# A fourth q/k buffer with earlier loads, the small constant added in another copy, and x sums spread over more periods

## The chip, the cores and the metric

One core of one Trainium2 chip. The metric is the device time of one execution in microseconds (us). The kernel before takes 1035.89 us, the median of three runs (1034.39, 1035.89, 1038.68).

## The reference

Attention over 4 batches, 8 heads, 576 tokens, head size 64, and behind it two gated layers on the 2304 x 512 result:

```python
scores = q @ k.T / 8 ; causal mask ; bias = min(-(cum[q] - cum[k]), 0), cum = cumsum(max(s, 0))
attn = exp(scores - rowmax) ; attn = attn / (sum(attn) + 1e-9) ; x = attn @ v
x = (sigmoid(x @ w_gate) * (x @ w_val)) @ w_out
out = ((x @ w_a) * (x @ w_b)) @ w_out2
```

The gated layers have 512 inputs and 1536 inner columns. Their weights arrive as float64 and are converted to float32 on the chip by integer operations.

## The kernel before, in words

The kernel has two stages. The first 207 us or so are attention (`attention()`), the rest are the two gated layers (`mlps()`). Each stage records its operations in a `Schedule` with a name, an engine, a duration, what it depends on, a due time ("prio") and, for some, a buffer that it takes and one that it gives back. The attention stage is emitted with `in_order=True`: of all operations whose predecessors have been emitted, the one with the lowest due time comes next. So the due times, in periods of `HT` = 6.1 us for one head, are an order written out by hand for every engine and for the DMA queues of SP (nc.sync), ACT (nc.scalar) and POOL (nc.gpsimd). An engine runs its instructions in that order and waits where an operand is not there yet. The second stage is emitted by a planner from its own durations; the change does not touch it, except that one operation of its first list (`rc`) is shorter.

For head i the operations that matter here are, with the lines of the profile:

- `lqk` (L380, SP): load q and k of the head, 288 KB, into `r_t[i % NR2]`; with three buffers it must wait until `hq1`, `hk1`, `lok` and `loq` of head i-3 have read the old contents.
- `hq1`, `hk1` (L532, L533, ACT): round q and k to the short format into `o_t[i % 4]`.
- `hk2` (L534, ACT's queue) and `hq2` (L535, SP's queue): copy the rounded k and q to the other half of the partitions, 144 KB each; the profile shows both as o<-o.
- `lok` (L536, DVE) and `loq` (L538, POOL): what rounding left of k and q. `lok` needs the transfer of `hk2`.
- `S` (L557, L562, PE): scores of the head in two groups, 0 and 1, one PSUM tile `ps_g` after the other. `mx` (L570, DVE): row maxima, which free `ps_g`. `mT` (L577, PE), `mc` (L579, ACT) and `md` (L581, ACT's queue): turn the maxima, copy them to `mr_t[i % 3]` and write them as a row of the operand.
- `ST` (L594, L595, PE): scores transposed, less the maximum. `ex` (L600, ACT): exponentials. `cs` (L616, POOL): the causal edge.

For two heads together (pair j): `lv` (L384, L385, SP) loads v; `pv` and `pd` (L641, L654, PE) are the product with v and the sums; `xc` (L663, ACT) and `dc` (L665, DVE) copy both out of PSUM; `dc` writes `dn`. Then the sums go through DRAM (`dw` L676, `dr` L677) into a small tile `t` of 128 x 12 (`sc` in the profile), `rc` adds 1e-9 (L669) and takes the reciprocal (L670), and `rd`, `rb`, `xm` (L682, POOL) and `xd` (L684) scale x and write it to `x_sb`. The last pairs' `dr` to `xd` run in the second stage.

Beside that the attention stage has the first weights to load and convert (`LOADS`: L194 on SP's queue, L215 on ACT, L216, L218, L220 and L223 on DVE; a tuple gives the period of each step) and their sums (L255), and it prepares the first x operands of the second stage: `xs` (L318, DVE) sums of x parts, `xh` (L321, ACT) their rounded half, `xl` (L324, DVE) the rest. `AT_S`, `AT_H` and `AT_L` give the period of each. Two staging tiles (`stg`) hold S1 to S4.

## Time and profile before

| | |
|---|---|
| median of three runs | 1035.89 us |
| the profiled execution, its own time | 1037.12 us |
| its span, first to last instruction | 1035.1 us |
| busy: PE, DVE, ACT, POOL | 1009.5, 700.1, 466.2, 385.4 us |
| mean granted TensorE clock | 0.995 of full speed |

The profiled execution is 1.23 us above the median, and 2.0 us of it lie around the span. Below, "PE" is TensorE, "DVE" VectorE, "ACT" ScalarE, "POOL" GpSimd and "SP" SyncE. In the timeline a row gives the start in us, the duration, the engine and line, the operation, its tiles, and in brackets how long the engine sat idle before it and what released it. A queue's own rows are named SPq and ACTq.

### The profile page before, as it was taken

To read this page: it belongs to the slowest core of one execution; us is meant where nothing else is said; L and a number is where in the kernel's file an instruction comes from. 1 tells how busy PE (TensorE), PEld (TensorE's weight loads), DVE (VectorE), ACT (ScalarE), POOL (GpSimd) and SP (SyncE) were. 2 spreads that over 40 slices of the span, in tenths; PEclk is the share of its full clock that TensorE was granted. 3 is DMA by queue.
4 is the path that set the end of the run, shared out by engine and by line. 5 is a ranking of instruction groups with operands and counts; after the bars stand their busy time and mean duration, and the time that the engine had idled before them with its cause. 6 is when DMAs were issued, how large, how long until landed. Compare 5 with 4: busy or idle time off the path is not lost.

```text
span 1035.1 us, 17118 instructions
## 1 busy us (share of the span) xinstructions
PE 1009.5 (98%) x6160; PEld 912.6 (88%) x6160; DVE 700.1 (68%) x1146; ACT 466.2 (45%) x891; POOL 385.4 (37%) x388
## 2 busy tenths in 40 slices
PE   6999899999999999999999999999999999999998
PEld 4777676699999999998888899999999999888886
DVE  7787789789689655679855339867876566932222
ACT  3676566465555445555343235334333334432221
POOL 5677688452356334433200013244533432400000
PEclk9999999999999999999999999999999999999999
DMA  5667778341234222445653332124432244544333
GB/s 158 184 172 206 192 190 198 100 152 67 103 128 139 91 102 84 163 165 199 207 157 98 121 129 92 58 90 142 128 103 87 102 154 171 179 137 137 112 103 102
DMA packets 93586, 139.76 MB, mean 135 GB/s; under 512 B 16215, under 2 KB 54863, under 8 KB 93502
## 3 DMA queue, kind: packets, MB, share of 16 engines
q1 hardware_dynamic: 89234, 133.03, 41.0%
q10 hardware_dynamic: 2988, 4.95, 1.8%
q0 software_dynamic: 1280, 0.70, 0.3%
q8 instruction: 48, 0.79, 0.3%
q14 instruction: 36, 0.29, 0.1%
HBM read 85.53 MB, written 33.45 MB: 115 GB/s over the span
## 4 chain that ended last, share of the span: by engine, by line
PE 79%; DVE 11%; DMA 5%; issue 2%; ACT 2%; POOL 1%; SPq 0%; ACTq 0%; DVEq 0%; POOLq 0%
PE ps L290 24%; PE ps L292 24%; PE ps L291 24%; PE ps_x L641 2%; DVE nm L570 2%; PE ps_g L557 2%; DMA vx<-in_vm_dram 2%; PE ps_x L654 1%; DMA o<-o 1%; DVE o L536 1%; DVE s L824 1%; DVE hs L318 1%; DVE rg L324 1%; ACT pt L600 1%; DMA r<-in_qk_dram 1%
## 5 line engine op out<-in xcount | busy, mean ns | idle before, releaser
L290 PE MATMUL ps<-rg,wk 128*128 128x384 f32 (+2 forms) x1128 | 381.9, 339 | 2.6 <-DVE s L824 2.6
L292 PE MATMUL ps<-rg,wk 128*128 128x384 f32 (+2 forms) x1128 | 381.0, 338 | 0.0
L290 PEld LDWEIGHTS ps<-rg,wk 128*128 128x128 f32 x1128 | 211.8, 188 | 9.0 <-DVE s L824 4.3
L292 PEld LDWEIGHTS ps<-rg,wk 128*128 128x128 f32 x1128 | 211.8, 188 | 3.8
L824 DVE TENSOR_TENSOR s<-ps,s 128x384 f32<-128x384 f32 x216 | 119.1, 553 | 114.4 <-PE ps L292 66.2
L291 PE MATMUL ps<-x_sb,wk 128*128 128x384 f32 x576 | 192.5, 334 | 0.0
L291 PE MATMUL ps<-rg,wk 128*128 128x384 f32 (+2 forms) x552 | 188.5, 341 | 0.0
L837 POOL TENSOR_TENSOR hs<-s,s 128x384 f32<-128x384 f32 x72 | 87.8, 1219 | 265.7 <-issue 92.9
L821 ACT COPY s<-ps 128x384 f32<-128x384 f32 x216 | 103.6, 480 | 182.6 <-PE ps L292 181.4
L268 POOL TENSOR_TENSOR wk<-raw,wk 128x512 fp32r<-128x512 f32 x96 | 125.3, 1332 | 148.0 <-DMA rg<-hd 101.8
L904 DVE TENSOR_TENSOR rg<-rg 128x512 fp32r<-128x512 f32 (+1 forms) x120 | 79.9, 670 | 111.4 <-ACT rg L903 108.5
L903 ACT CAST rg<-rg 128x512 fp32r<-128x512 f32 (+1 forms) x120 | 68.6, 578 | 146.1 <-DMA rg<-hd 113.3
L291 PEld LDWEIGHTS ps<-x_sb,wk 128*128 128x128 f32 x576 | 108.1, 188 | 0.1
L291 PEld LDWEIGHTS ps<-rg,wk 128*128 128x128 f32 x552 | 103.7, 188 | 3.6
L570 DVE TENSOR_REDUCE nm<-ps_g 128x1 f32<-128x512 f32 (+4 forms) x154 | 74.1, 531 | 19.6 <-PE ps_g L562 19.0
L290 PE MATMUL ps<-rg,rg 128*128 128x512 f32 (+1 forms) x228 | 86.1, 378 | 0.0
L291 PE MATMUL ps<-rg,rg 128*128 128x512 f32 (+1 forms) x228 | 86.1, 378 | 0.0
L292 PE MATMUL ps<-rg,rg 128*128 128x512 f32 (+1 forms) x228 | 86.1, 378 | 0.0
L215 ACT ACTIVATE mag<-raw 128x512 f32<-128x512 f32 x72 | 48.4, 673 | 55.2 <-DVE raw L223 31.4
L220 DVE SCALAR_TENSOR_TENSOR raw<-raw,u 128x512 int32<-128x512 int32 x72 | 62.5, 868 | 4.1
L218 DVE SCALAR_TENSOR_TENSOR u<-raw,u 128x512 int32<-128x512 int32 x72 | 60.8, 844 | 1.5
L616 POOL TENSOR_SCALAR_AFFINE_SELECT pt<-pt 128x256 f32<-128x256 f32 (+1 forms) x96 | 42.0, 458 | 52.9 <-ACT pt L600 49.3
(120 smaller groups left out, 1503.0 us busy)
## 6 DMA issues: line engine op xcount, KB each, us to landing
hd<-hs SPq DMA_DIRECT2D x72, 384.0 KB
rg<-hd SPq DMA_DIRECT2D x72, 256.0 KB
raw<-in_moe_w_out_dram SPq DMA_DIRECT2D x24, 512.0 KB
r<-in_qk_dram SPq DMA_DIRECT2D x32, 288.0 KB
rg<-hd SPq DMA_DIRECT2D x72, 128.0 KB
raw<-in_moe_w_gate_dram SPq DMA_DIRECT2D x12, 512.0 KB
raw<-in_moe_w_val_dram SPq DMA_DIRECT2D x12, 512.0 KB
raw<-in_moe_w_a_dram SPq DMA_DIRECT2D x12, 512.0 KB
```

The source lines that it names most:

```text
L218: ("DVE", 0.65, lambda: nc.vector.scalar_tensor_tensor(out=u, in0=parts(n, m)[1], scalar=-0x40000000, in1=u, op0=ALU.bitwise_and, op1=ALU. ...
L220: ("DVE", 0.65, lambda: nc.vector.scalar_tensor_tensor(out=parts(n, m)[1], in0=parts(n, m)[0], scalar=29, in1=u, op0=ALU.logical_shift_rig ...
L268: return lambda: nc.gpsimd.tensor_tensor(out=wcols(n, a, w, 1), in0=src(), in1=f32(wcols(n, a, w, 0)), op=ALU.subtract)
L290: nc.tensor.matmul(out=outp, lhsT=wh, rhs=xh, start=start and e == 0, stop=False, skip_group_check=True)
L291: nc.tensor.matmul(out=outp, lhsT=wh, rhs=xl, start=False, stop=False, skip_group_check=True)
L292: nc.tensor.matmul(out=outp, lhsT=wl, rhs=xh, start=False, stop=stop and e == n - 1, skip_group_check=True)
L570: nc.vector.tensor_reduce(out=nm[0:n, c:c + 1], in_=ps[0:n, p0:p0 + nk], axis=AX.X, op=ALU.max)
L821: op((x,) + key, "ACT", ACT_P, lambda x=x: nc.scalar.copy(out=s(x), in_=bank("X")), [P(p)], end(p) - 10, acq=("s", key + (x,)))
L824: return lambda: nc.vector.tensor_tensor(out=s(x), in0=bank(b_), in1=s(x), op=ALU.add)
L837: op(("h2",) + key, "Pool", PTT, lambda: nc.gpsimd.tensor_tensor(out=half(1), in0=s("s4"), in1=s("s2"), op=ALU.mult), [("c22",) + key, (g[ ...
L903: op(("hh",) + key, "ACT", 0.17 + 0.00083 * N, lambda hs=hs, N=N: nc.scalar.copy(out=hs()[:, 0, 0:N], in_=f32(hs()[:, 1, 0:N])), [("hl",) ...
L904: op(("ho",) + key, "DVE", 0.157 + 0.00104 * N, lambda hs=hs, N=N: nc.vector.tensor_tensor(out=hs()[:, 1, 0:N], in0=f32(hs()[:, 1, 0:N]), ...
```

## The change

q and k get four load buffers, and from head 3 on the load is due one period (6.1 us) earlier; the loads of heads 3 and 4 stand at the same place near the start. `mr_t` goes from three tiles to two, so `mc` of a head waits for `md` of two heads before. `dc` becomes an addition of 1e-9 on its way out of PSUM, and the addition in `rc` is dropped. The last conversion step of one weight piece (L223) moves from period 27 to 26; the sum S2 moves from 27.1 to 28, its rounded half from 28 to 29 and its rest from 29 to 31.01; A22's rounded half from 29 to 28; S1's rest from 28 to 29; S4's rounded half from 30.1 to 31 and A12's from 31 to 30.

```diff
@@ -349,7 +349,7 @@
             SUP = 1.0 / scale
             R1 = D + 2 * NR
             KB = R1 + 2
-            NO, NR2, NX, NPT = 4, 3, 4, 4
+            NO, NR2, NX, NPT = 4, 4, 4, 4
             QD, QV = 384, 128
             P0 = [0, 576, 1024, 1344, 1536]
             CQ1, CK1 = 0, 640
@@ -368,7 +368,7 @@
             mkb = tile1([128, 448], BF16, "mkb")
             nm_t = [tile1([128, 8], FP32, f"nm{i}") for i in range(4)]
             stg = [tile1([128, 2 * NP], FP32, f"stg{i}") for i in range(2)]
-            mr_t = [tile1([NC, 128], F32R, f"mr{i}") for i in range(3)]
+            mr_t = [tile1([NC, 128], F32R, f"mr{i}") for i in range(2)]
             o_t = [tile1([128, CK1 + S], F32R, f"o{i}") for i in range(NO)]
             p_t = [tile1([128, 2 * S], F32R, f"o2_{i}") for i in range(3)]
             rel = tile1([128, 2, S], F32R, "rel")
@@ -491,7 +491,7 @@
             op("mkb", "ACT", 0.7, masks_b, ["masks"], -280)
             op("mkc", "ACT", 0.2, masks_c, ["mkb"], -279)
             op("busy", "PE", 8.0, busy, ["mkb"], -270, acq=("F", "busy"), rel=("F", "busy"))
-            for j in range(NR2):
+            for j in range(3):
                 op(("lqk", j), "SP", 0.6, lambda j=j: load_qk(j), ["s"], (-290, -259.5, -258.5)[j], lat=3.0)
             for j in range(NO):
                 op(("sel", j), "SP", 1.3, lambda j=j: selectors(o_t[j]), ["selc"] + [("ms", j) if j < 3 else "more"] * (j > 0), (-260, -257, -208, 0.5)[j], lat=2.2)
@@ -520,25 +520,25 @@
                 b, h = divmod(i, H)
                 t0 = HT * i
                 o, o2, r, pt = o_t[i % NO], p_t[i % 3], r_t[i % NR2], pt_t[i % NPT]
-                nm, mr = nm_t[i % 4], mr_t[i % 3]
+                nm, mr = nm_t[i % 4], mr_t[i % 2]
                 k1, q1, k2, q2 = o[:, CK1:CK1 + S], o[:, CQ1:CQ1 + S], o2[:, S:2 * S], o2[:, 0:S]
                 up, dn = slice(0, D), slice(D, 2 * D)
                 done = [("ST", i - NO, c) for c in range(NC)] + [("S", i - NO, g) for g in range(2)]
                 done2 = [("ST", i - 3, c) for c in range(NC)]
 
-                if i >= NR2:
+                if i >= 3:
                     op(("lqk", i), "SP", 0.7, lambda: load_qk(i),
-                       [(w, i - NR2) for w in ("hq1", "hk1", "lok", "loq")], t0 - 4 * HT + 3.9, lat=3.0)
-                op(("hq1", i), "ACT", 0.65, lambda: nc.scalar.copy(out=q1[up], in_=r[up]), [("lqk", i)] + done, (-251, -247, -209.7)[i] if i < NR2 else t0 - 3 * HT + 5.2)
-                op(("hk1", i), "ACT", 0.65, lambda: nc.scalar.copy(out=k1[up], in_=r[dn]), [("lqk", i)] + done, (-251, -247, -209.7)[i] if i < NR2 else t0 - 3 * HT + 5.22)
-                op(("hk2", i), "ACT", 0.7, lambda: nc.scalar.dma_start(out=f32(k2[dn]), in_=f32(k1[up])), [("hk1", i)] + done2, (-209.8, -209.6, -8.55)[i] if i < NR2 else t0 - 2 * HT + 0.35)
-                op(("hq2", i), "SP", 0.5, lambda: nc.sync.dma_start(out=f32(q2[up]), in_=f32(q1[up])), [("hq1", i)] + done2, (-208.5, -207.5, -206)[i] if i < NR2 else t0 - 2 * HT + 0.1)
+                       [(w, i - NR2) for w in ("hq1", "hk1", "lok", "loq")], max(t0 - 5 * HT + 3.9, 0.01 * i - 2.23), lat=3.0)
+                op(("hq1", i), "ACT", 0.65, lambda: nc.scalar.copy(out=q1[up], in_=r[up]), [("lqk", i)] + done, (-251, -247, -209.7)[i] if i < 3 else t0 - 3 * HT + 5.2)
+                op(("hk1", i), "ACT", 0.65, lambda: nc.scalar.copy(out=k1[up], in_=r[dn]), [("lqk", i)] + done, (-251, -247, -209.7)[i] if i < 3 else t0 - 3 * HT + 5.22)
+                op(("hk2", i), "ACT", 0.7, lambda: nc.scalar.dma_start(out=f32(k2[dn]), in_=f32(k1[up])), [("hk1", i)] + done2, (-209.8, -209.6, -8.55)[i] if i < 3 else t0 - 2 * HT + 0.35)
+                op(("hq2", i), "SP", 0.5, lambda: nc.sync.dma_start(out=f32(q2[up]), in_=f32(q1[up])), [("hq1", i)] + done2, (-208.5, -207.5, -206)[i] if i < 3 else t0 - 2 * HT + 0.1)
                 op(("lok", i), "DVE", 0.9, lambda: nc.vector.tensor_tensor(
                     out=k2[up], in0=r[dn], in1=f32(k2[dn]), op=ALU.subtract), [("hk2", i)], (-8.7, -8.3)[i] if i < 2 else t0 - HT - 0.3)
                 op(("loq", i), "DVE" if i < 2 else "Pool", 0.9 if i < 2 else 1.4, lambda: (nc.vector if i < 2 else nc.gpsimd).tensor_tensor(
                     out=q2[dn], in0=r[up], in1=f32(q1[up]), op=ALU.subtract), [("hq1", i)] + done2, -151 + 2 * i if i < 2 else t0 - HT + 1.45)
 
-                if i >= NR2:
+                if i >= 3:
                     op(("rel", i), "SP", 0.5, lambda: nc.sync.dma_start(out=f32(q1[R1:KB + 1]), in_=relq_d[i]), relst + done, t0 - 3 * HT + 0.05, lat=2.2)
                     op(("relk", i), "Pool", 0.6, lambda: nc.gpsimd.dma_start(out=f32(k1[D:R1]), in_=f32(rel[i:NR * BH:BH])), ["sums"] + done, t0 - 3 * HT + 1.4, lat=2.2)
 
@@ -571,13 +571,13 @@
                                 out=nm[0:n, c:c + 1], in_=ps[0:n, p0:p0 + nk], axis=AX.X, op=ALU.max)
 
                     op(("S", i, g), "PE", (0.7, 0.65)[g], scores,
-                       [("rel", i), ("hq1", i), ("hk1", i), ("sel", i % NO), "mkc", "pads"] + [("relk", i)] + ([("relq", i, j) for j in range(NR)] if i < NR2 else []),
+                       [("rel", i), ("hq1", i), ("hk1", i), ("sel", i % NO), "mkc", "pads"] + [("relk", i)] + ([("relq", i, j) for j in range(NR)] if i < 3 else []),
                        first_at[g] if first_at and first_at[g] else t0 + (3.5 - 2 * HT, -HT)[g], acq=to)
                     op(("mx", i, g), "DVE", (1.4, 1.1)[g], maxima, [("S", i, g), ("mT", i - 4), "pads"], (first_at[g] or 6.1) + 0.05 if first_at else t0 + (4.3 - 2 * HT, 0.7 - HT)[g], rel=to)
                 op(("mT", i), "PE", 0.15, lambda: nc.tensor.transpose(sc.get("t", ("m", i))[0:NC, 0:128], nm[:, 0:NC], idf),
                    [("mx", i, 0), ("mx", i, 1), "masks"], (-8.7, -8.4)[i] if i < 2 else t0 - HT + 3.4, acq=("t", ("m", i)))
                 op(("mc", i), "ACT", 0.25, lambda: nc.scalar.copy(out=mr, in_=sc.get("t", ("m", i))[0:NC, 0:128]),
-                   [("mT", i), ("md", i - 3)], (-8.7, -8.4)[i] + 0.05 if i < 2 else t0 - HT + 3.55, rel=("t", ("m", i)))
+                   [("mT", i), ("md", i - 2)], (-8.7, -8.4)[i] + 0.05 if i < 2 else t0 - HT + 3.55, rel=("t", ("m", i)))
                 op(("md", i), "ACT", 0.4, lambda: nc.scalar.dma_start(
                     out=f32(o[KB:KB + 1, CQ1:CQ1 + 640]), in_=f32(mr)), [("mc", i)] + done, (-8.7, -8.4)[i] + 0.06 if i < 2 else t0 - HT + (3.93, 5.21)[i % 2], lat=2.2)
 
@@ -662,11 +662,10 @@
                 for u, (a, z) in enumerate(((0, QV), (QV, S))):
                     op(("xc", j, u), "ACT", (0.2, 0.5)[u], lambda a=a, z=z: nc.scalar.copy(out=x[:, a:z], in_=sc.get(*pxk)[:, QD + a:QD + z]),
                        [("pv", j, u), ("xd", j - NX)], t0 + (4 - u * (j < NH // 2 - 1)) * HT + 3.9)
-                op(("dc", j), "DVE", 0.5, lambda: nc.vector.tensor_copy(out=dn, in_=sc.get(*pxk)[:, 0:QD]),
+                op(("dc", j), "DVE", 0.5, lambda: nc.vector.tensor_scalar(dn, sc.get(*pxk)[:, 0:QD], 1e-9, None, ALU.add),
                    [("pd", j), ("dw", j - 1), ("xc", j, 0), ("xc", j, 1)], t0 + 4 * HT + 5.7, rel=pxk)
 
                 def recip():
-                    nc.vector.tensor_scalar(t, t, 1e-9, None, ALU.add)
                     nc.vector.reciprocal(out=t, in_=t)
 
                 def spread():
@@ -690,7 +689,7 @@
             for n in [("xm", LATE - 1), ("xd", LATE - 1)] + [(k, j) for j in range(LATE, NH // 2) for k in ("dr", "rc", "rd", "rb", "xm", "xd") if (k, j) != ("dr", LATE)]:
                 late[n] = sc.ops.pop(n)
 
-            LOADS = [(0.02, 2, 2.5, 3, 4), (2, 4, 5, 6, 7), (5, 8, 10, 11, 12), (12, 14, 15, 16, 17), (14, 17, 20, 21, 22), (21, 23, 24, 25, 27)]
+            LOADS = [(0.02, 2, 2.5, 3, 4), (2, 4, 5, 6, 7), (5, 8, 10, 11, 12), (12, 14, 15, 16, 17), (14, 17, 20, 21, 22), (21, 23, 24, 25, 26)]
             SUMS = [(8, 9, 9), (18, 19, 18)]
             for e, (ld, ab, *dv) in enumerate(LOADS):
                 n, m = e // 2, e % 2
@@ -706,9 +705,9 @@
             rg = lambda: region[0]
             get = lambda name: sc.get("stg", name)
             done = [("xd", j) for j in range(H)]
-            AT_S = {"S1": 25, "S3": 26, "S2": 27.1, "S4": 30}
-            AT_H = {"A11": 25, "S3": 26.1, "S1": 27, "S2": 28, "A22": 29, "S4": 30.1, "A12": 31}
-            AT_L = {"S3": 27, "S1": 28, "A11": 31.02, "S2": 29, "A22": 31.25, "A12": 32, "S4": 31.2}
+            AT_S = {"S1": 25, "S3": 26, "S2": 28, "S4": 30}
+            AT_H = {"A11": 25, "S3": 26.1, "S1": 27, "A22": 28, "S2": 29, "A12": 30, "S4": 31}
+            AT_L = {"S3": 27, "S1": 29, "A11": 31.02, "S2": 31.01, "A22": 31.25, "A12": 32, "S4": 31.2}
             for k, (name, p, q, _) in enumerate(XS):
                 op(("xs", name), "DVE", 0.96, x_sum(nc.vector, get, 0, k), done + [("xs", z) for z in (p, q) if z[0] == "S"] + [("xs", "S3")] * (name == "S4"),
                    HT * AT_S[name] + 0.9, acq=("stg", name))
```

## Rows read from the trace of the kernel before

**Rows 1.** Busy time of each engine in both stages and in three short stretches:
```profile
core 0: us, PE busy (x) PEld busy (x) DVE busy (x) ACT busy (x) POOL busy (x), PEclk, DMA share, GB/s
0.00:207.33 207.33, 188.13 (x1769) 141.79 (x1769) 168.35 (x307) 124.86 (x248) 142.91 (x201) 0.98 0.66 175
207.33:1035.10 827.77, 821.37 (x4396) 770.79 (x4392) 531.79 (x839) 341.35 (x643) 242.53 (x188) 1.00 0.38 125
...
110.00:120.00 10.00, 10.00 (x62) 7.74 (x62) 7.29 (x15) 6.03 (x13) 6.17 (x8) 0.83 0.69 201
180.00:190.00 10.00, 10.00 (x87) 7.46 (x78) 7.00 (x13) 4.78 (x10) 6.22 (x7) 0.85 0.47 140
189.00:208.00 19.00, 17.88 (x218) 13.10 (x217) 13.08 (x18) 8.15 (x18) 8.94 (x13) 1.00 0.30 83
```

**Rows 2.** Timeline of DVE: the first maxima of heads 5, 9, 17, 19, 28 and 31:
```profile
35.47 1.35 DVE L570 TENSOR_REDUCE nm<-ps_g 128x1 f32<-128x512 f32 x3 [0.46 <-PE ps_g L562]
...
57.12 1.35 DVE L570 TENSOR_REDUCE nm<-ps_g 128x1 f32<-128x512 f32 x3 [0.89 <-PE ps_g L562]
...
102.92 1.35 DVE L570 TENSOR_REDUCE nm<-ps_g 128x1 f32<-128x512 f32 x3 [0.48 <-PE ps_g L562]
...
118.19 1.35 DVE L570 TENSOR_REDUCE nm<-ps_g 128x1 f32<-128x512 f32 x3 [1.11 <-PE ps_g L562]
...
168.31 1.35 DVE L570 TENSOR_REDUCE nm<-ps_g 128x1 f32<-128x512 f32 x3 [0.23 <-PE ps_g L562]
...
189.11 1.35 DVE L570 TENSOR_REDUCE nm<-ps_g 128x1 f32<-128x512 f32 x3 [0.58 <-PE ps_g L562]
```

**Rows 3.** Who waited for whom from 57 to 190 us: total, times, longest:
```profile
ACT o L532 <- DMA r<-in_qk_dram: 13.9, 8, 3.5
...
DVE o L536 <- DMA o<-o: 6.7, 5, 3.6
```

**Rows 4.** DVE's groups of instructions from 57 to 190 us, by shape:
```profile
L669 DVE TENSOR_SCALAR sc<-sc 128x12 f32<-128x12 f32 x11 | 9.8, 893 | 0.1
...
L665 DVE COPY dn<-ps_x 128x384 f32<-128x384 f32 x11 | 6.0, 548 | 0.0
```

**Rows 5.** Timeline of POOL and DVE around one addition of 1e-9:
```profile
127.70 1.69 POOL L538 TENSOR_TENSOR o<-r,o 64x576 fp32r<-64x576 f32 x1
...
128.03 1.40 DVE L669 TENSOR_SCALAR sc<-sc 128x12 f32<-128x12 f32 x1
```

**Rows 6.** Timeline of ACT and DVE at the first large stall:
```profile
98.21 0.67 ACT L532 CAST o<-r 64x576 fp32r<-64x576 f32 x1 [1.20 <-DMA r<-in_qk_dram]
...
106.48 0.67 ACT L532 CAST o<-r 64x576 fp32r<-64x576 f32 x1 [3.53 <-DMA r<-in_qk_dram]
...
107.89 0.75 DVE L536 TENSOR_TENSOR o<-r,o 64x576 fp32r<-64x576 f32 x1 [3.62 <-DMA o<-o]
```

**Rows 7.** The chain of work that ended last, at the same place (start, us, what):
```profile
99.76 8.04 DMA o<-o
```

**Rows 8.** Timeline of DVE and PE at the second large stall:
```profile
172.56 0.69 DVE L223 SCALAR_TENSOR_TENSOR raw<-mag,raw 128x512 f32<-128x512 f32 x1
...
174.36 0.96 DVE L318 TENSOR_TENSOR stg<-stg,x_sb 128x768 f32<-128x768 f32 x1
...
175.23 1.38 DVE L669 TENSOR_SCALAR sc<-sc 128x12 f32<-128x12 f32 x1
...
178.13 0.65 PE L557 MATMUL ps_g<-o 128*128 128x256 f32 x3 [2.42 <-DVE nm L570]
```

**Rows 9.** Timeline of ACT near the end of the attention stage:
```profile
194.71 0.83 ACT L321 CAST rg<-stg 128x768 fp32r<-128x768 f32 x1 [2.90 <-DVE stg L318]
```

**Rows 10.** Timeline of DVE and PE near the start:
```profile
27.33 1.08 DVE L570 TENSOR_REDUCE nm<-ps_g 128x1 f32<-128x256 f32 x2 [0.27 <-PE ps_g L562]
...
28.56 0.27 PE L577 MATMUL ps_t<-idf,nm 128*5 128x128 f32 x1 [1.26 <-ACT pt L600]
```

**Rows 11.** Timeline of ACT: the row of maxima of head 7 is issued, head 9's copy:
```profile
52.58 0.71 ACTq L581 DMA_DIRECT2D o<-mr  x1
...
62.01 0.24 ACT L579 CAST mr<-ps_t 5x128 fp32r<-5x128 f32 x1
```

## The prediction

> **What bounds the kernel now.** I read the busy time by stage first. In the second stage PE is busy for 821.37 of 827.77 us; in the attention stage for 188.13 of 207.33 us, so 19.2 us of its idle time lie here [rows 1]. All edits but one small instruction of the second stage touch the attention stage, so the question is how much of those 19 us they give back.
>
> Next comes the pace. The reader is to see in the timeline of DVE when each head's first maxima start: heads 5 to 9 take 57.12 - 35.47 = 21.65 us, 5.41 us a head [rows 2]. I take this as the floor that PE sets: the four heads before any weight work weighs on DVE. From head 9 to head 31 the kernel needs 189.11 - 57.12 = 131.99 us for 22 heads, and at 5.41 us they would need 119.1. The excess of 12.9 us splits by the same rows: heads 9 to 17 2.50 us (45.80 against 43.30), heads 17 to 19 4.45 (15.27 against 10.82), heads 19 to 28 1.41 (50.12 against 48.71), heads 28 to 31 4.56 (20.80 against 16.24) [rows 2]. Three causes stand in the profile:
>
> The loads of q and k come late: ACT waits for them 8 times, 13.9 us in all, and with it wait the exponentials and the transfers behind them in its order [rows 3]. DVE stands behind other work: the addition of 1e-9 on 12 elements takes 0.89 us in the mean [rows 4], because it stretches to the end of the POOL instruction that runs beside it (128.03 + 1.40 = 129.43 against 127.70 + 1.69 = 129.39) [rows 5]. And the granted clock: after each of the two long stalls a stretch at 1.2 instead of 2.4 GHz follows, which leaves 0.83 and 0.85 of full clock in a 10 us slice, so 1.7 and 1.5 us of PE's work are lost there [rows 1].
>
> **The change part by part.**
>
> *Fourth buffer, loads one period sooner.* No transfer is added. In the steady state SP issues one such load a period at the same place of its order as before, only for the next head; what it waits for there (POOL's `loq`) keeps its place too. A load thus gains one period, 5.41 us, and the longest wait for it is 3.53 us [rows 6], so ACT's waits should go, unless POOL and not the load releases some. Only at the start one load moves ahead of others in SP's queue (a small read of `relq_d`, a weight piece, two selector transfers). I cost that at 0: PE's step at 28.56 us follows maxima that DVE ends at 28.41 (27.33 + 1.08), so an earlier ACT gains 0.15 us at most, and I know of no reader of the pushed transfers that waits here [rows 10]. Bounds: 1 us lost, 1.3 us gained (the whole 1.26 us wait of that row).
>
> Where the stall goes, heads 17 to 19: two waits end together there, ACT's for q and k at 106.48 and DVE's for the transfer of rounded k, which was issued at 99.76 and took 8.04 us, at 107.89 [rows 6, 7]. The first vanishes. The second starts sooner: ACT had waited 1.20 us just before issuing it [rows 6], and issued that much earlier it stands ahead of the next q/k and v loads instead of behind them. DVE was ready at 107.89 - 3.62 = 104.27, so the transfer may take 4.5 us from 99.76, or 5.7 from 98.56, without a stall. I take it as nearly gone, with its clock loss, and leave 1.0 us: gain 4.45 - 1.0 = **3.5 us**. Next late there is this transfer.
>
> *Addition in the copy.* It removes 11 additions, 9.8 us of DVE, between 57 and 190 us [rows 4], and makes 11 copies (0.548 us each, PSUM source) into additions. The trace shows no addition out of PSUM. Lower bound: as the copy, 0. Upper bound: it stretches as the removed one did, to 1.40 us [rows 5], 0.85 us more each. I take 0, because the copy is the nearest in source, shape and engine: its mean of 0.548 over 11 shows none of that stretching [rows 4]. Where DVE was behind, the removal returns what the excess shows, and no more: heads 9 to 17 2.50 us, which also hold part of the waits for q and k; I leave 0.5, so **2.0 us**; heads 19 to 28 1.41, I leave 0.2, so **1.2 us**.
>
> *x sums spread.* Around 175 us DVE does a conversion step of 0.69, a rest, a sum of 0.96 and the addition of 1.38 us before the maxima that PE waits for, and PE idles 2.42 us [rows 8]. Three of the four leave: 0.69 + 0.96 + 1.38 = 3.03, more than the 2.42. The step of 0.69 lands one period earlier, where DVE had 0.23 us free before head 28's maxima [rows 2]: 0.46 us late, which I charge in full. The sum changes places with another of its kind a period later. So of 4.56 us, the clock loss included, **4.1 us** come back. Bounds: nothing below 1.4 us, the removed addition alone, and 4.56.
>
> *The end of the stage.* ACT waits 2.90 us for a sum that its rounding of S4 needs, at 194.71, and behind it stand the copies that PE needs; PE idles 19.00 - 17.88 = 1.12 us from 189 to 208 us [rows 1, 9]. Afterwards the rounding of A12, which needs no such sum, has that place. **1.1 us**. The later rests of S1 and S2 are hidden: DVE is busy 13.08 of those 19 us [rows 1].
>
> *Two tiles for the row of maxima.* The copy of head 9 would now wait for the row of head 7, issued 9.4 us before (52.58 to 62.01) [rows 11]; the longest transfer seen in this stage takes 8.04 [rows 7]. 0.
>
> Sum: 3.5 + 2.0 + 1.2 + 4.1 + 1.1 = 11.9 us. The profiled execution took 1037.12 us, so 1025.2 by its own time; it lies 1.2 us above the median of 1035.89, from which the sum gives 1024.0. I forecast 1024.5.
>
> **The rivals.**
>
> *The transfer stall stays.* The 8.04 us of the transfer of rounded k [rows 7] may be the traffic of all queues and not its place: issued 1.20 us earlier it ends 1.20 us earlier, DVE waits 2.4 of the 3.62 us, and the low clock follows again. Then heads 17 to 19 give 1.2 us instead of 3.5, and about 1 us of the others stays: 8.6 us, 1027.3. For it speaks that DVE waits for such transfers five times [rows 3]; against it that four of the five share the 6.7 - 3.6 = 3.1 us that are left. The Trainium skill (DMA: Bandwidth & Descriptors, section on queues, rings and completion order) says that each DMA engine takes the queues in turn, packet by packet, so that SP's loads could not simply stand ahead of ACT's transfer; by that rule this rival holds. The 8.04 us for 144 KB neither show nor exclude it.
>
> *The new addition stretches like the old.* Then 11 times 0.85 us, 9.4 us, come onto DVE in place of the 9.8 taken off, and its backlog stays: the 2.0 and 1.2 us don't come back, and of the 4.1 only what the moving gives, 4.1 - 1.4 = 2.7. Left are 3.5 + 2.7 + 1.1 = 7.3 us, 1028.6. Against it stand the 0.548 us of the copy.
>
> *The loads did not matter.* ACT's and DVE's waits could be cover for one another everywhere, with PE's real floor higher than 5.41 us. Then only the end and a little come back: 2 us, 1034. Against it is the even pace of heads 5 to 9 with the same PE work.
>
> *Slower.* With a faster pace the same bytes must flow in less time (the DMA engines are busy 0.66 of the stage already [rows 1]), and the transfer of rounded k becomes late in every second head, where the v load stands beside it. It decides once such a transfer takes more than the 4.5 us above. If 11 of them cost half of the 3.62 us each, 1.8, that is 19.9 us against the 11.9: 8 us slower, 1044. Against it: 5 of 22 heads show such a wait now [rows 3], the longest of them right behind a late load [rows 6].
>
> **How the numbers follow.** About 0.5% (5.2 us) is what a measurement of this kernel can tell from no change. Chances: the forecast 0.56, the transfer stall staying 0.16, the new addition stretching 0.08, the loads not mattering 0.13, slower 0.07. The first three lie beyond 5.2 us: faster 0.80, same 0.13, slower 0.07. The range starts at 1020.5: all of the excess and of the idle end, 12.9 + 1.1, and 1.3 at the start come to 15.3 below the median. It ends at 1032: the third case, 1028.6, with some 3 us for the bounds above that went against the sum (1 us lost at the start, and 4.1 - 1.4 = 2.7 at the x sums, not both in full); it leaves out the last two cases, 0.20.
>
> **What would show it.** Right: ACT's waits for q and k of rows 3 gone, no addition on the 12-element tile, the new one at 0.55 us, PE without the 2.42 us gap, no stretch at 1.2 GHz behind 100 us, heads 9 to 31 in 119 to 122 us, the second stage unchanged. Wrong: L536's waits for o<-o grown, L665 above 0.6 us in the mean, or a pace that stays at 6 us a head.

## The result and the profile after

| | before | after |
|---|---|---|
| median of 12 runs | 1036.49 us | 1028.23 us |
| lowest and highest | 1034.36, 1044.91 | 1025.77, 1036.06 |
| profiled execution, its own time | 1037.12 | 1028.64 |
| its span | 1035.1 | 1026.9 |

The ratio is 0.9913, 95% interval 0.9888 to 0.9938: faster by 8.3 us by the medians and by 9.0 by the ratio, where the prediction's sum had 11.9. The time lies in its range and 3.7 us above its number. Executions of one kernel differ by some 10 us here, so a stage of one profile is itself uncertain by one or two us; more on that below.

Busy time by stage after the change. The cut at 199.33 us stands right before the first matmul of L290, as the one at 207.33 us did in [rows 1]:

```profile
0.00:199.33 199.33, 185.80 (x1768) 140.27 (x1768) 161.18 (x293) 125.48 (x248) 146.08 (x201) 0.98 0.68 182
199.33:1026.90 827.57, 821.38 (x4396) 770.90 (x4392) 530.04 (x837) 340.80 (x643) 243.22 (x188) 1.00 0.38 125
```

The second stage is what it was (827.57 against 827.77 us). The attention stage is 8.0 us shorter, and PE's idle time in it fell from 19.2 to 13.5 us.

The first maxima of heads 5, 9, 17, 19, 28 and 31, in the timeline of DVE after the change, against [rows 2]:

```profile
35.86 1.35 DVE L570 TENSOR_REDUCE nm<-ps_g 128x1 f32<-128x512 f32 x3 [1.68 <-PE ps_g L562]
...
57.52 1.35 DVE L570 TENSOR_REDUCE nm<-ps_g 128x1 f32<-128x512 f32 x3 [1.31 <-PE ps_g L562]
...
103.38 1.35 DVE L570 TENSOR_REDUCE nm<-ps_g 128x1 f32<-128x512 f32 x3 [0.98 <-PE ps_g L562]
...
114.65 1.35 DVE L570 TENSOR_REDUCE nm<-ps_g 128x1 f32<-128x512 f32 x3 [1.76 <-PE ps_g L562]
...
165.91 1.34 DVE L570 TENSOR_REDUCE nm<-ps_g 128x1 f32<-128x512 f32 x3
...
182.46 1.34 DVE L570 TENSOR_REDUCE nm<-ps_g 128x1 f32<-128x512 f32 x3
```

Heads 17 to 19 take 11.27 us instead of 15.27 and heads 28 to 31 take 16.55 instead of 20.80. Heads 9 to 17 take what they took (45.86 against 45.80), and heads 19 to 28 take 1.1 us more (51.26 against 50.12). Before the maxima of heads 28 and 31 DVE was not idle: there it is behind.

Who waited for whom from 57 to 190 us after the change (total, times, longest), against [rows 3]:

```profile
DVE o L536 <- DMA o<-o: 2.5, 4, 1.0
...
ACT o L532 <- DMA r<-in_qk_dram: 0.9, 2, 0.6
```

ACT's waits for q and k went from 13.9 to 0.9 us, DVE's for the transfer of rounded k from 6.7 to 2.5. DVE's groups of the same stretch, against [rows 4]:

```profile
L665 DVE TENSOR_SCALAR dn<-ps_x 128x384 f32<-128x384 f32 x12 | 6.6, 546 | 0.0
...
L669 DVE RECIPROCAL sc<-sc 128x12 f32<-128x12 f32 x11 | 2.4, 220 | 0.1
```

The addition in the copy costs 0.546 us, as the plain copy did (0.548), and 9.8 us of small additions are gone.

What is late now, in the timeline of PE, POOL and DVE at heads 25, 27 and 28:

```profile
147.42 0.74 PE L557 MATMUL ps_g<-o 128*128 128x512 f32 x3 [0.95 <-DMA o<-rel]
...
157.45 1.85 POOL L538 TENSOR_TENSOR o<-r,o 64x576 fp32r<-64x576 f32 x1
157.94 1.91 DVE L220 SCALAR_TENSOR_TENSOR raw<-raw,u 128x512 int32<-128x512 int32 x1
...
159.90 1.28 DVE L570 TENSOR_REDUCE nm<-ps_g 128x1 f32<-128x512 f32 x3
...
163.67 1.77 POOL L538 TENSOR_TENSOR o<-r,o 64x576 fp32r<-64x576 f32 x1
164.06 1.92 DVE L223 SCALAR_TENSOR_TENSOR raw<-mag,raw 128x512 f32<-128x512 f32 x1
```

L223 took 0.69 us in its old place [rows 8] and takes 1.92 in its new one: it starts 0.39 us after POOL's subtraction and ends 0.54 us behind that one's end (164.06 + 1.92 = 165.98 against 163.67 + 1.77 = 165.44). The maxima of head 28 follow at once. And at head 25 PE waits for a transfer of `rel` that POOL issues.

### The profile page after: what moved, and what is told of

Its sections match the earlier page's. It is cut to its first block, busy times and chain, and to the rows that moved or that the text cites. A ratio compares the mean times of both kernels' runs of the same rounds, so it can differ in the third digit from the quotient of the medians.

```text
span 1026.9 us, 17097 instructions
## 1 busy us (share of the span) xinstructions
PE 1007.2 (98%) x6160; PEld 911.2 (89%) x6160; DVE 691.2 (67%) x1130; ACT 466.3 (45%) x891; POOL 389.3 (38%) x388
## 3 DMA queue, kind: packets, MB, share of 16 engines
q10 hardware_dynamic: 2988, 4.95, 2.0%
## 4 chain that ended last, share of the span: by engine, by line
PE 82%; DVE 7%; DMA 4%; issue 2%; ACT 1%; POOL 1%; SPq 1%; ACTq 0%; DVEq 0%; POOLq 0%
PE ps L290 24%; PE ps L291 24%; PE ps L292 24%; PE ps_x L641 2%; PE ps_g L557 2%; PE ps_x L654 1%; PE ps_e L594 1%; PE ps_e L595 1%; DVE nm L570 1%; DVE s L823 1%; DMA o<-o 1%; DVE raw L220 1%; DVE u L218 1%; DVE u L216 1%; DMA raw<-in_moe_w_val_dram 1%
## 5 line engine op out<-in xcount | busy, mean ns | idle before, releaser
L290 PE MATMUL ps<-rg,wk 128*128 128x384 f32 (+2 forms) x1128 | 382.1, 339 | 2.5 <-DVE s L823 2.4
L290 PEld LDWEIGHTS ps<-rg,wk 128*128 128x128 f32 x1128 | 211.9, 188 | 8.8 <-DVE s L823 4.5
L268 POOL TENSOR_TENSOR wk<-raw,wk 128x512 fp32r<-128x512 f32 x96 | 127.5, 1355 | 147.1 <-ACT wk L265 131.8
L290 PE MATMUL ps<-rg,rg 128*128 128x512 f32 (+1 forms) x228 | 86.2, 378 | 0.0
L215 ACT ACTIVATE mag<-raw 128x512 f32<-128x512 f32 x72 | 48.3, 671 | 57.1 <-DVE raw L223 31.1
L220 DVE SCALAR_TENSOR_TENSOR raw<-raw,u 128x512 int32<-128x512 int32 x72 | 63.4, 881 | 4.1
L831 ACT ACTIVATE s<-s 128x384 f32<-128x384 f32 x72 | 37.9, 527 | 52.0 <-DVE s L823 51.8
```

What stands on the lines that cost most here:

```text
L220: ("DVE", 0.65, lambda: nc.vector.scalar_tensor_tensor(out=parts(n, m)[1], in0=parts(n, m)[0], scalar=29, in1=u, op0=ALU.logical_shift_rig ...
L268: return lambda: nc.gpsimd.tensor_tensor(out=wcols(n, a, w, 1), in0=src(), in1=f32(wcols(n, a, w, 0)), op=ALU.subtract)
L290: nc.tensor.matmul(out=outp, lhsT=wh, rhs=xh, start=start and e == 0, stop=False, skip_group_check=True)
```

## The experiments

**One part at a time.** Three kernels carry one part of the diff each, put on the kernel before.

```diff
-            NO, NR2, NX, NPT = 4, 3, 4, 4
+            NO, NR2, NX, NPT = 4, 4, 4, 4
...
-  ... t0 - 4 * HT + 3.9, lat=3.0)
+  ... max(t0 - 5 * HT + 3.9, 0.01 * i - 2.23), lat=3.0)
```

> The kernel before with the q and k part alone (fourth buffer, loads one period sooner, two mr tiles). My theory, that the stage by stage difference of the two traces is the sum of independent parts: the stall and the half clock at heads 17 to 19 go (4.0 us of the 8.2 that the span lost), heads 9 to 17 keep their pace (45.8 us between the first maxima), heads 28 to 31 keep their 20.8 us, so 1032 to 1033 us, and no PE stretch at 1.2 GHz after 100 us. Rival one, that the loads don't matter and the addition made room on VectorE: 1035.5 to 1036.5 us, with the stall still there. Rival two, the recorded sum's size (3.5 at heads 17 to 19, about 1 in heads 9 to 17, some of the end of the stage): 1031 to 1032 us and heads 9 to 17 in 44 to 45 us.

Measured: 0.9999 (0.9970 to 1.0028). The waits of ACT for q and k are gone (1.3 us left from 57 to 190 us) and heads 17 to 19 take 10.75 us, yet no gain shows in the time. Both my theory and the prediction's sum fall for the part alone; rival one has the time, but not the stall that it wanted.

```diff
-  nc.vector.tensor_copy(out=dn, in_=sc.get(*pxk)[:, 0:QD]),
+  nc.vector.tensor_scalar(dn, sc.get(*pxk)[:, 0:QD], 1e-9, None, ALU.add),
...
-                    nc.vector.tensor_scalar(t, t, 1e-9, None, ALU.add)
```

> The kernel before with the addition alone (1e-9 added in the copy of the sums out of PSUM, the 12-element addition gone). My theory, that VectorE doesn't set the pace in heads 9 to 28 and the addition sat in idle time: 1035.8 to 1036.8 us, heads 9 to 17 in 45.5 to 46.2 us. Rival, the recorded sum's size: the addition removed gives back about 1.5 us of the waits of heads 9 to 28: 1034.5 to 1035.2 us. Rival on the other side, that the copy with an addition holds the PSUM tile longer: above 1037 us with a mean of L665 over 0.60 us.

Measured: 0.9972 (0.9949 to 0.9994), which is 2.9 us where I expected none; the rival of the recorded sum's size (0.998 to 0.999) fits.

```diff
-  ... (21, 23, 24, 25, 27)]
+  ... (21, 23, 24, 25, 26)]
...
-  AT_S = {"S1": 25, "S3": 26, "S2": 27.1, "S4": 30}
+  AT_S = {"S1": 25, "S3": 26, "S2": 28, "S4": 30}
```

> The kernel before with the x sums alone (S2's sum and three of the low and high parts moved to other periods, the last weight step from period 27 to 26). My theory, that it gives the whole gain of heads 28 to 31 (20.8 to 16.6 us) and the gain of the end of the stage (1.3), and loses about 1 us in heads 24 to 28 by the moved weight step: 1031.5 to 1032.8 us. Rival, that the waits of heads 28 to 31 come from late q and k loads too, so that without the fourth buffer the period is long again: heads 28 to 31 above 18.5 us, and 1033.5 to 1035 us.

Measured: 0.9974 (0.9948 to 1.0000). Heads 28 to 31 take 17.27 us although ACT waits 14.1 us for q and k as before, so the late loads don't make the long stretch there. But the x sums alone didn't make it either. The kernel with the addition alone has them all in their old places, and in its timeline of DVE heads 28 to 31 take 187.24 - 170.05 = 17.19 us:

```profile
170.05 1.35 DVE L570 TENSOR_REDUCE nm<-ps_g 128x1 f32<-128x512 f32 x3 [0.21 <-PE ps_g L562]
...
176.36 0.22 DVE L669 RECIPROCAL sc<-sc 128x12 f32<-128x12 f32 x1
...
187.24 1.35 DVE L570 TENSOR_REDUCE nm<-ps_g 128x1 f32<-128x512 f32 x3 [1.88 <-PE ps_g L562]
```

The x sums moved away or the addition of 1.38 us gone [rows 8]: in these profiles either is enough. The profiled execution with the x sums alone took 1038.41 us, 2.3 above its median.

**One part left out.** The three single parts come to 0.1 + 2.9 + 2.7 = 5.7 us, the whole to 9.0 us by the ratio. So each part was taken out of the kernel after. First the x sums' part:

```diff
-  AT_S = {"S1": 25, "S3": 26, "S2": 28, "S4": 30}
+  AT_S = {"S1": 25, "S3": 26, "S2": 27.1, "S4": 30}
...
```

> The kernel after without the x sums' new places (q and k part and addition stay). Theory A, that the four us which the q and k part gains at heads 17 to 19 are given back where the x sums stand (there VectorE's long steps are stretched beside GpSimd's), so that the q and k part is worth its gain only together with the new places: a ratio of 0.996 to 1.000 to the kernel before, heads 24 to 31 in 43 us or more. Theory B, that the parts' effects multiply (the kernel with the q and k part alone came to 0.9999, with the addition alone to 0.9972): 0.9971, heads 24 to 31 in 41 to 43 us.

Measured: 0.9942 (0.9918 to 0.9967). Theory A is out: without the x sums' new places the other two are worth 6 us, and heads 24 to 31 take 22.25 + 18.12 = 40.4 us. Theory B's 0.9971 lies just outside the interval too, but it is worked out from two ratios that are uncertain themselves. Then the addition's:

```diff
+                    nc.vector.tensor_scalar(t, t, 1e-9, None, ALU.add)
...
```

> The kernel after without the addition's move (q and k part and x sums stay). Theory A, that q and k part and x sums need each other and are the whole gain, and the addition is worth nothing by itself: a ratio of 0.990 to 0.993 to the kernel before, heads 17 to 19 in about 11 us and heads 28 to 31 in 16.5 to 17 us. Theory B, that the parts' effects multiply (0.9999 with the q and k part alone, 0.9974 with the x sums alone): 0.997.

Measured: 0.9962 (0.9938 to 0.9986). Theory A is out here too: taking the addition's part out loses 5 us of the 9. Theory B's 0.997 lies in the interval. Last the q and k part:

```diff
-            NO, NR2, NX, NPT = 4, 4, 4, 4
+            NO, NR2, NX, NPT = 4, 3, 4, 4
...
```

> The kernel after without the q and k part (addition and x sums stay). Theory A, that the waits for q and k come back and take what the x sums would give: 0.995 to 0.998 of the kernel before, ScalarE's copies of q and k (L532) waiting some 14 us for their loads in heads 9 to 28. Theory B, that the parts' effects multiply (0.9972 and 0.9974): 0.9946. If it comes to 0.992 or less, the q and k part gives nothing even in company.

Measured: 0.9941 (0.9921 to 0.9961), with 14.3 us of ACT's waits back. This is the value of the multiplied effects; the upper end of theory A's range (0.995 to 0.998) is out, its lower end isn't.

Each part's worth now stands in four pairs of kernels that differ in it alone (ratio without it minus ratio with it, in us of 1036.5):

| part | alone | beside the one | beside the other | beside both | mean |
|---|---|---|---|---|---|
| q and k | 0.1 | addition: 3.1 | x sums: 1.2 | 2.9 | 1.8 |
| addition | 2.9 | q and k: 5.9 | x sums: 3.4 | 5.1 | 4.3 |
| x sums | 2.7 | q and k: 3.8 | addition: 3.2 | 3.0 | 3.2 |

Each ratio is uncertain by some 0.0025, so a difference by about 3.7 us and a mean of four by about 1.8 (written +- 1.8 below). By the means the addition, the smallest edit, gave most; that order is not settled.

**The stages by repeats.** Up to head 24 the kernels with and without the x sums' part issue the same instructions in the same order. Their profiles are repeats of one another, and head 9 to head 24 can be compared with a spread (starts of the first maxima of both heads, us):

| q and k | addition | heads 9 to 24 | mean |
|---|---|---|---|
| no | no | 89.13, 88.90 | 89.0 |
| yes | no | 85.56, 86.46 | 86.0 |
| no | yes | 89.00, 84.89 | 86.9 |
| yes | yes | 83.87, 85.32, 82.78 | 84.0 |

(The 82.78 is the kernel with the step in period 27, below.) Together the two parts give back 5.0 us here, and no profile with both is within 3.5 us of one with neither. The same nine profiles at heads 17 to 19: 15.27 and 12.84 with neither, 12.23 and 12.27 with the addition alone, 10.75 to 11.58 with the fourth buffer. Two kernels below are thinned only from head 23 on and are repeats up to there: 12.43 without the fourth buffer, 10.79 with it. So the 15.27 on which the prediction rests is the largest of five samples of that stall, and only in this profile of the five does a stretch at 1.2 GHz follow it (0.83 of full clock from 110 to 120 us [rows 1]).

**Where the gain of q and k alone went.** From head 24 to the last copy of the sums (L665) the kernel before takes 208.23 - 146.25 = 61.98 us, the one with q and k alone 207.21 - 143.41 = 63.80. PE's waits for DVE's maxima in 39 us of these periods (total, times, longest) are, before,

```profile
PE ps_g L557 <- DVE nm L570: 2.4, 1, 2.4
```

and with q and k alone

```profile
PE ps_g L557 <- DVE nm L570: 4.6, 2, 2.7
```

Against my expectation the granted clock falls there too: to 1.2 GHz behind a wait of PE that ends at 163.5 us, which leaves 0.83 of full clock from 160 to 170 us. The timeline of DVE and POOL with q and k alone:

```profile
172.63 1.57 POOL L538 TENSOR_TENSOR o<-r,o 64x576 fp32r<-64x576 f32 x1
172.85 2.17 DVE L324 TENSOR_TENSOR rg<-stg,rg 128x768 fp32r<-128x768 f32 x1
174.28 2.02 POOL L682 TENSOR_TENSOR xt<-xt,rb 128x576 f32<-128x576 f32 x1
175.06 2.06 DVE L318 TENSOR_TENSOR stg<-stg,x_sb 128x768 f32<-128x768 f32 x1
```

Both DVE steps run beside POOL's subtraction and product; the same L318 took 0.96 us before [rows 8]. To test whether running beside POOL, and not the amount of work, makes them long, POOL's two products were thinned in the last periods:

```diff
-  out=q2[dn], in0=r[up], ...
+  out=q2[dn] if i < 23 else q2[dn][:, 0:32], in0=r[up] if i < 23 else r[up][:, 0:32], ...
...
-  out=x, in0=x, in1=rb, op=ALU.mult
+  out=x if j < 7 else x[:, 0:32], in0=x if j < 7 else x[:, 0:32], in1=rb if j < 7 else rb[:, 0:32], op=ALU.mult
```

> The kernel before with the q and k part alone, and GpSimd's two products thinned to 32 of their 576 columns, for q's low part from head 23 on and for the attention's result from pair 7 on; that part of the computation is left out. Theory A, that the q and k part's gain was given back at heads 24 to 31 because VectorE's long steps run beside GpSimd's there (L220 1.91, L324 2.17, L318 2.06 us): these steps fall to 0.7 to 1.2 us, heads 24 to 31 take 40 to 42 us instead of 44.7, and the time is 3 to 4 us below the kernel with the q and k part alone, a ratio of 0.996 to 0.997. Theory B, that these periods are long by the amount of work or by late transfers: heads 24 to 31 stay above 43.5 us and the ratio is 0.999 to 1.0.

Measured: 0.9891 (0.9863 to 0.9919, 4 runs), more than I expected, and heads 24 to 31 in 22.99 + 17.27 = 40.26 us. PE's waits for DVE's maxima from 140 to 206 us fall from 4.6 to 0.5 us. DVE's groups by shape from 143 to 206 us, first with q and k alone:

```profile
L669 DVE TENSOR_SCALAR sc<-sc 128x12 f32<-128x12 f32 x6 | 3.6, 593 | 0.1
...
L318 DVE TENSOR_TENSOR stg<-stg,x_sb 128x768 f32<-128x768 f32 x1 | 2.1, 2065 | 0.0
L220 DVE SCALAR_TENSOR_TENSOR raw<-raw,u 128x512 int32<-128x512 int32 x1 | 1.9, 1909 | 0.0
```

and then with POOL thinned (the mean of one, in ns, behind the comma):

```profile
L669 DVE TENSOR_SCALAR sc<-sc 128x12 f32<-128x12 f32 x6 | 1.3, 211 | 0.1
...
L318 DVE TENSOR_TENSOR stg<-stg,x_sb 128x768 f32<-128x768 f32 x1 | 1.0, 960 | 0.0
L220 DVE SCALAR_TENSOR_TENSOR raw<-raw,u 128x512 int32<-128x512 int32 x1 | 0.7, 744 | 0.0
```

The same instructions are 0.4 to 1.2 us shorter, and nothing of DVE was changed. That POOL's company stretches them is shown. How much of the time comes from it isn't: thinning also shortens POOL's own work, and no run separates the two. The control is the same thinning without q and k:

> The kernel before with GpSimd's two products thinned as in the run with the q and k part (32 of 576 columns, q's low part from head 23 on, the attention's result from pair 7 on); that part of the computation is left out. With the q and k part the thinning came to 0.9891. Theory A, that the q and k part does give back the stall at heads 17 to 19 and that GpSimd's company at heads 24 to 31 took it away again: without that part the same thinning leaves the late loads in place, 0.992 to 0.995, with ScalarE's L532 still waiting 13 us or more for r and a long interval somewhere in heads 9 to 24. Theory B, that the thinning alone makes the gain and the q and k part nothing: 0.988 to 0.990.

Measured: 0.9958 (0.9933 to 0.9983); theory B is out. With POOL thinned the q and k part is worth 0.9958 - 0.9891 = 0.0067, some 7 us, uncertain by about 3.9, against 0.1 us without. In the two profiles it is 2.6 us (spans of 1028.4 and 1025.8 us), all of it at heads 9 to 24; the control's profile is its fastest execution. So the part is worth something once POOL is out of the way, and how much stays open. The waits for q and k stand there as before (total, times, longest):

```profile
ACT o L532 <- DMA r<-in_qk_dram: 16.0, 11, 2.7
```

**What made the addition cost so much.** Two more reciprocals of the same 12 elements stand in its place:

```diff
                     nc.vector.reciprocal(out=t, in_=t)
+                    nc.vector.reciprocal(out=t, in_=t)
+                    nc.vector.reciprocal(out=t, in_=t)
```

> The kernel after with two more reciprocals of the same 12 elements behind the one that is there (1/(1/(1/x))), some 0.23 us each: where the addition stood, VectorE has more instructions again, but of the form that the trace of after never shows longer than 0.229 us. Theory A, that the addition cost so much because it was stretched beside GpSimd (0.16 to 1.40 us, 0.77 in the mean before): a ratio of 0.989 to 0.993 to the kernel before, as the kernel after (0.9913). Theory B, that any instruction at this place of VectorE's order, or of the chain from the sums to the reciprocal's transfer, costs: 0.995 to 0.997, as the kernel after with the addition back in its old place (0.9962).

Measured: 0.9921 (0.9890 to 0.9953), as the kernel after; the end of the interval just reaches theory B. DVE's groups from 57 to 200 us (L671 is the last of the three):

```profile
L671 DVE RECIPROCAL sc<-sc 128x12 f32<-128x12 f32 x14 | 3.2, 228 | 0.5
L669 DVE RECIPROCAL sc<-sc 128x12 f32<-128x12 f32 x14 | 3.1, 219 | 0.1
```

Two instructions more, 0.46 us for every two heads, and no loss to be seen. Together with the 593 against 211 ns above this speaks for the stretching as the addition's price, and not its place; the intervals alone don't settle it.

**The weight step back in period 27.** Alone of the change's edits, this one is undone:

```diff
-  ... (21, 23, 24, 25, 26)]
+  ... (21, 23, 24, 25, 27)]
```

> The kernel after with one thing undone: the last weight step (L223) back in period 27. Theory A, that in period 26 it is stretched to 1.9 us beside GpSimd and delays the maxima of head 28 (165.91 us), which costs 0.8 to 1.1 us of the span: 1027.0 to 1027.6 us, with heads 24 to 28 in 23.3 to 23.8 us where the kernel after takes 24.5. Theory B, that period 27 is as full and the step only moves its delay from head 28 to head 29: within 0.3 us of the kernel after, with heads 28 to 31 longer by what heads 24 to 28 get back.

Measured: 0.9870 (0.9833 to 0.9907, 6 runs). L223 and the sum behind it are short in the timeline of DVE, and the maxima of head 28 find DVE idle:

```profile
163.79 1.35 DVE L570 TENSOR_REDUCE nm<-ps_g 128x1 f32<-128x512 f32 x3 [0.70 <-PE ps_g L562]
...
167.42 0.75 DVE L223 SCALAR_TENSOR_TENSOR raw<-mag,raw 128x512 f32<-128x512 f32 x1
168.09 0.95 DVE L324 TENSOR_TENSOR rg<-stg,rg 128x768 fp32r<-128x768 f32 x1
```

Heads 24 to 28 take 22.75 us instead of 24.52, somewhat more gained than theory A's 23.3 to 23.8, and heads 28 to 31 stay at 16.60, as it has it. Of the 1.8 us the step has 1.06: heads 27 to 28 take 163.79 - 158.84 = 4.95 instead of 165.91 - 159.90 = 6.01. The rest is the wait for `rel` at head 25, where both kernels issue the same instructions and only the profile after shows it. It is the fastest of all kernels here by its median, 1025.99 us, 13 us below the kernel before that was timed beside it. Its interval overlaps that of the kernel after, and the two were timed on different chips, so that it beats the kernel after is likely and not shown.

**Moving POOL's work instead.** From the kernel with the step in period 27, POOL's subtraction goes ahead of the causal selections:

```diff
-  ... -151 + 2 * i if i < 2 else t0 - HT + 1.45)
+  ... -151 + 2 * i if i < 2 else t0 - HT + 0.45)
```

> The kernel after with the last weight step back in period 27 and GpSimd's low part of q (L538) ahead of the causal selections of its period instead of behind them, so that it runs where GpSimd waits for ScalarE's exponentials and no longer beside the weight steps and x sums. Theory A, that VectorE's long steps were stretched by L538 and that this sets the period there: L220 and L324 mostly back to 0.7 to 1.0 us, 1021 to 1025 us, a ratio of 0.983 to 0.987. Theory B, that L538 then stretches VectorE's other subtraction (L536) instead and delays the selections: 0.988 to 0.995. Slower than the kernel before only if the selections become the bound, which the waits of PE's products for them would show.

Measured: 0.9979 (0.9955 to 1.0002), a miss for theory A and worse than B. L220 takes 1.75 us in the mean from 57 to 200 us instead of 1.02 in the kernel with the step in period 27, and L536, which theory B expected to stretch, 1.00 instead of 1.11. The company moved instead of going away; in the timeline of DVE and POOL:

```profile
80.84 3.58 DVE L220 SCALAR_TENSOR_TENSOR raw<-raw,u 128x512 int32<-128x512 int32 x1
81.17 1.42 POOL L681 TENSOR_TENSOR xt<-xt,rb 128x576 f32<-128x576 f32 x1
82.54 1.31 POOL L268 TENSOR_TENSOR wk<-raw,wk 128x512 fp32r<-128x512 f32 x1
```

Here two POOL instructions follow one another, and the DVE step that began before them ends behind both (82.54 + 1.31 = 83.85, and 80.84 + 3.58 = 84.42).

**One transfer fewer.** Also from that kernel:

```diff
-  for e in range(2):
-      nc.sync.dma_start(out=rb[e * D:(e + 1) * D], in_=rr_d[j, e, 0:S][None].to_broadcast([D, S]))
+  nc.sync.dma_start(out=rb, in_=rr_d[j, :, 0:S][:, None].to_broadcast([2, D, S]))
```

> The kernel after with the last weight step back in period 27 and the two transfers of a pair's reciprocals to the partitions merged into one of the same bytes, one transfer fewer per pair on SP's queue. Theory A, that the number of transfers in flight limits when ScalarE and SP may issue the next ones: 0.5 to 2 us below the kernel with the step in period 27 alone (0.987), a ratio of 0.985 to 0.9865. Theory B, that bytes and places set the transfers' times: 0.987 within its interval, 0.9855 to 0.9885, with ScalarE's waits behind L581 and L534 unchanged.

Measured: 1.0560 (1.0525 to 1.0595), 58 us slower than before, outside both theories. The merged transfer is slow: issued at 111.70, it lets POOL go on at 123.06 us. The timeline of SP's and ACT's queues shows who else pays:

```profile
111.70 0.58 SPq L672 DMA_DIRECT2D rb<-rr_d  x1
111.92 0.72 ACTq L581 DMA_DIRECT2D o<-mr  x1
112.33 0.52 SPq L194 DMA_DIRECT2D raw<-in_moe_w_gate_dram  x1
113.69 0.35 SPq L380 DMA_DIRECT2D r<-in_qk_dram  x1
114.72 0.38 SPq L384 DMA_DIRECT2D vx<-in_vm_dram  x1
115.15 1.73 SPq L385 DMA_DIRECT2D vx<-in_vt_dram  x1
115.92 0.51 ACTq L534 DMA_DIRECT2D o<-o  x1
116.98 0.42 SPq L542 DMA_DIRECT2D o<-relq_d  x1
123.00 0.50 SPq L535 DMA_DIRECT2D o<-o  x1
```

The eighth transfer behind it (L535, rounded q) is issued 6 us behind the one before it, when the slow one has landed, and the queue's own waits from 57 to 223 us name it:

```profile
SPq L674 <- DMA rb<-rr_d: 38.6, 7, 6.0
...
SPq L535 <- DMA rb<-rr_d: 9.5, 2, 5.5
```

Neither L674 (sums to DRAM) nor L535 touches rb. The trace shows the link: in this stretch the transfers of these two queues report their completion on eight semaphores in turn, L535 gets the one that the slow transfer had (number 108), and SP waits for it before it issues L535. So the run says nothing on whether one transfer fewer would help, because it also made the transfer slow; it shows that a slow transfer blocks later ones of other data.

## Why the prediction was right, and where not

**The floor and the stage**: right in what they gave. The second stage is unchanged, and PE's idle time in the attention stage paid for the gain. The reason given for the floor doesn't hold: weight steps do run on DVE between heads 5 and 9. But DVE still idles before the maxima there, as in this stretch of the timeline before:

```profile
38.87 0.84 DVE L223 SCALAR_TENSOR_TENSOR raw<-mag,raw 128x512 f32<-128x512 f32 x1
40.53 1.35 DVE L570 TENSOR_REDUCE nm<-ps_g 128x1 f32<-128x512 f32 x3 [0.82 <-PE ps_g L562]
```

**Heads 17 to 19, 3.5 us**: the two profiles give 4.0, and the causes named are gone. That the two agree is partly luck, since the stall of the profile read was the largest of five. By the repeats some 2.0 us is the fairer size (13.0 us in the mean of the five without the fourth buffer, 11.0 of the six with it). The silent step that a gain of this stage stays isn't borne out either: with the part alone 3.6 us are gained at heads 9 to 24, 1.8 us are lost from head 24 on, where DVE's long steps ran beside POOL's products, and the time shows none.

**Heads 9 to 17, 2.0, and 19 to 28, 1.2 us**: in the two profiles nothing and 1.1 us lost. The repeats mend the first: with both parts heads 9 to 24 are 5.0 us shorter, against 3.5 + 2.0 and a part of the 1.2. Of the loss in heads 19 to 28, 1.06 us are L223, and 0.95 the wait for `rel`, which the kernel with the step in period 27, the same up to there, doesn't show.

**The x sums, 4.1 us, and the end of the stage, 1.1**: in the two profiles 4.25 and, from head 31's maxima to the last copy of the sums, 19.12 - 17.78 = 1.34. The rows of these copies, before and after:

```profile
208.23 0.56 DVE L665 COPY dn<-ps_g 128x384 f32<-128x384 f32 x1 [3.98 <-ACT xt L663]
...
200.24 0.56 DVE L665 TENSOR_SCALAR dn<-ps_g 128x384 f32<-128x384 f32 x1 [4.19 <-ACT xt L663]
```

The 1.1 is sound: with POOL not thinned, this end takes 19.1 us in all four profiles without the x sums' part and 17.6 to 18.1 in all seven with it (the kernel with the merged transfer aside). The 4.1 is not the moving's own. The prediction gave 1.4 of it to the removed addition and 2.7 to the moving, but in the profile with the addition's part alone heads 28 to 31 take 17.19 us, 3.6 below the kernel before. By the medians of four pairs the x sums are worth 3.2 +- 1.8 us, end included. Mis-sized is also the moved step: "0.46 us late, which I charge in full". It was costed at the 0.69 us that it took beside no POOL instruction, and it took 1.92 beside one, which made head 28 1.06 us late.

**The addition**: its pricing by the PSUM copy, 0.548 us, was right (0.546), which rules out the rival that it stretches. What it was to give is 2.0 + 1.2 and the 1.4 inside the x sums, 4.6 in all, and the medians say 4.3 +- 1.8. The q and k part was to give the 3.5, and measured 1.8 +- 1.8. So part by part the sum holds within the noise, with q and k at its edge.

**Start and mr tiles, 0**: head 9's maxima stand at 57.1 to 61.6 us with and without the part, in no order.

**The rivals.** By the number alone the first two (1027.3 and 1028.6) are nearer to 1028.2 than the forecast; the rows decide. The transfer stall did not stay (L536 2.5 us instead of 6.7), and after the change every 10 us of the attention stage behind 30 us has the full granted clock (1.00). That the loads don't matter fits the time of them alone and not the kernels beside the addition. A slowdown by late k transfers did not come. Of the signs named, heads 9 to 31 in 119 to 122 us failed: 124.94 in the profile after, 122.13 with the step in period 27.

So the sum, 11.9 against 8.3 us measured, was near because the three causes were the right ones. Of the 3.6 us between them 0.6 are the moved step (1.06 against 0.46) and some 1.5 the stall's size (3.5 against 2.0); the rest is within what single profiles scatter. What stands clear of the scatter is 5.0 us at heads 9 to 24, by q and k and the addition together, and some 1.4 us at the end of the stage, by the x sums. How the remainder of the gain divides at heads 24 to 31 stays open: the profiles give 39.4 to 44.7 us there.

## What to carry to other kernels

A step's duration in a profile holds only beside the work it ran beside: before moving one, look at which POOL instruction will run in its new place and price it at the longest form seen, not the shortest. A wait that a change removes may have been the spacing that kept two engines apart (argued here, not shown), so test parts alone and left out, and use the profiles of kernels that agree up to a point as repeats of that stretch. A tiny instruction whose longest duration is over eight times its shortest, as the addition's was, deserves a look before a large one that is steady.

## What was not expected of the hardware

Which POOL instruction DVE's steps run beside is worth as much as the whole change: moving POOL's subtraction alone cost some 11 us (0.9979 against 0.9870). One 12-element TENSOR_SCALAR takes 0.16 to 1.40 us in the kernel before, a RECIPROCAL of the same 12 elements never over 0.23. The 128x384 addition from PSUM takes 0.54 to 0.56 in the kernel after, and L220, with two SBUF inputs, 0.68 us at its shortest and 3.58 at its longest, with POOL's subtraction moved. The Trainium skill (SBUF — State Buffer, section "Who interferes with whom") says that VectorE and GpSimd share a pair of ports which one instruction holds alone, and that VectorE needs it for two SBUF inputs and for tensor_scalar in its two-port modes. The rows agree, and the thinned run shows the stretching by 593 against 211 ns; the ports themselves no run here shows.

The merged transfer moves the bytes of the two (288 KB) and took over 11 us, from its issue at 111.70 to POOL's start at 123.06. The Trainium skill (DMA: Bandwidth & Descriptors, section "Rules for kernel authors") says that an outermost dimension of few entries confines a transfer to at most as many DMA engines; the merged one has an outermost dimension of 2. The slow transfer agrees with it; how many engines carried it no run here shows.
